# A fused attention and mixture-of-experts kernel: list scatters between splits, the first early list read sooner, mask made on chip, decays spread by TensorE, states ahead of transposes in steps 1 and 2

## The chip, the cores and the metric

The kernel runs on one core of a Trainium2 chip. The metric is the device time of one execution in microseconds (us), the median of the runs. TensorE is PE in the profile (its weight loads PEld), VectorE is DVE, ScalarE is ACT, GpSimd is POOL, and SyncE, which issues most of the DMAs, is SP. A shape such as 128x512 is partitions by elements.

## What is computed

Retention attention with a decay per head, and on its output a mixture of 16 experts in 4 groups, one expert for each token.

```python
# attention: B, H, S, D = 4, 8, 768, 64
gamma = 1 - 2.0 ** (-5 - arange(H)); scale = 1 / sqrt(D)
for t in range(S):
    state = gamma * state + outer(k[:, :, t], v[:, :, t])   # D x D a head
    y[:, :, t] = scale * q[:, :, t] @ state
# experts: x = y as (3072 tokens, 512); 4 groups of 4 experts, 512 -> 1024 -> 512
g = argmax(x @ w_group); e = argmax(x @ w_expert[g])        # and their softmax weights
out[token] = g_w * e_w * (relu(x[token] @ w1[g, e]) @ w2[g, e])
```

## The kernel before

**Attention.** The 768 positions of each of 4 sequences are 6 chunks of 128. Two sequences are worked on together, so there are 12 steps (`i`, 0 to 11), each with two halves `u`, one a sequence. A step computes scores (`score_mm`, L232, into the four PSUM banks `sh`), masks them with a triangle (`score_mask`, L244, `pf<-sh,cst`), scales the values (`vprep`, L191, POOL, `vs<-lv,cst`), transposes the keys of the next step on PE (`keys_mm`, L217), and accumulates in PSUM banks `op` the old state's part (`state_out`, L283) and the chunk's own part (`value_out`, L296). The state grows in `stp` (`state_mm`, L258). `out_x` (L308) multiplies by the decays `gx` of each position, and `trans_mm` (L342) turns the result so that it can be stored in DRAM as `xd`. `logits_mm` (L316) and `select_mm` (L329) give the router's logits.

**Routing.** Every second step a `route` of four chunks runs on DVE in small operations (L381 to L475), with ranks from PE (L429, L431). For each chunk an indirect DMA from POOL (`enlist`, L481, `meta<-src,slot`, a scatter) then writes 128 pairs of token and weight into the experts' lists in DRAM.

**Early experts.** Experts 0 (`ua`) and 1 (`va`) start before all tokens are routed: their first 128 tokens come out of the first 12 and 16 chunks. Their weights are loaded in 256 KB parts (`wload_part`, L666) and split in two 16-bit parts, `wh` on ACT (L678) and `wl` on POOL or DVE (L680). `listed` reads the list back (L693, `mt<-meta`), `gather` fetches the tokens (L703, `xg<-xd,mt`), `xtrans` turns them on PE (L721, `tpx`), and `layers` multiplies (L769 and on). After the attention PE works on `ua` while the last route runs, then on `va`, on the rest of both lists (`ub`, `vb`), and on the 14 other experts, the order of which is known only from the whole routing.

**What sets the order.** The program is in a manual schedule: each engine's instructions stand as the Python code emits them, and each queue is in order. `attention` writes a step out by hand; it calls `beside(i, place)` at places -1, 0, 2, 4, 1, 3 of step `i`, and `extra(i)` at its end, and these put the work for the early experts between. The table `NEXT` says at which place of which step the parts of `va`'s weights are loaded. `entries(n)` scatters the next `n` chunks.

**The start.** SP issues the first half of q, k and v, then the constants `cst` (the mask of 256 columns, the value scales, the step decays), then the second halves and the next steps' loads, among them the decays `gx<-dec` of 128x512. PE runs nine warming matmuls (L153), and after the first scores two more (`heat`, L171).

Of the kernel before, what the change touches and what calls it, by code (L numbers as in the profile page):

```python
# [22 lines left out]
P = 128  # L23
# [24 lines left out]

C_TRI, C_GV, C_GS, C_REST = 0, 256, 304, 308
C_STRI, C_DESC, C_SEL = 0, 128, 148  # L50
# [18 lines left out]
def constants():  # L69
    s = np.arange(P)  # L70
    g = 1.0 - 2.0 ** (-5.0 - np.arange(H))
    c = np.zeros((P, C_REST + C_END), np.float64)
    for i in range(2):
        c[:, C_TRI + i * P:C_TRI + i * P + P] = (s ^ (64 * i))[:, None] <= s[None, :]

    n = np.arange(NC)[None, :, None] * P + KEYS.T[:, None, :] + 1.0
    c[:, C_GV:C_GV + NC * H] = (g ** -n).reshape(P, NC * H)
    for half in range(2):
        c[64 * half:64 * half + 64, C_GS:C_GS + 4] = g[[h[half] for h in HEAD]] ** P
    d = c[:, C_REST:]  # L80
    d[:, C_STRI:C_STRI + P] = s[:, None] < s[None, :]
    d[:, C_DESC:C_DESC + 20] = [4, 3, 2, 1] * 5
    d[:, C_SEL:C_SEL + 20] = s[:, None] % 32 == np.arange(20)[None, :]
    d[:, C_SEG:C_SEG + NP] = np.arange(NP) * CAP
    d[:, C_KP:C_KP + NP] = np.arange(NP)
    d[:, C_WP:C_WP + NP] = PW
    d[:, C_IT:C_IT + MAXI] = np.arange(MAXI)
    return c.astype(np.float32)


def decays():
# [3 lines left out]
    a = g[:, :, None] ** (np.arange(P) + 1.0) * (XS / np.sqrt(D))  # L95
    return np.repeat(a.transpose(1, 0, 2)[:, None], D, 1).reshape(P, DM).astype(np.float32)


KX = (4, 6)
NEXT = {(9, 0): (0, 2), (9, 3): (2, 4), (10, 0): (4, 8), (11, 0): (8, 12)}  # L100
KEYED = (9, 10)


class Kernel:
    def __init__(self, tc, qkv, kt, wr, w1p, w2p, cst, dec, out):
# [3 lines left out]
        self.st = {}  # L109
        self.todo = []  # L110
        self.steps = []
        self.held = None
# [7 lines left out]
    def setup(self):  # L120
# [7 lines left out]
        self.load("v", 0, (0,))  # L128
        nc.sync.dma_start(self.cst, self.a_cst[:, 0:C_REST])
        act = cp.tile([P, 1], F32, name="act")  # L130
        nc.scalar.activation(act, self.ones[:, 0:1], AF.Copy)
        self.ident = cp.tile([P, P], F32, name="ident")
        make_identity(nc, self.ident)

        self.sh = [self.pp.tile([P, 512], F32, name=f"sh{i}", tag="big", bufs=3) for i in range(3)]
# [4 lines left out]
        nc.vector.memset(self.wr, 0.0)  # L140
        self.gx = cp.tile([P, NC, 4, P], F32, name="gx")
        self.stri = cp.tile([P, P], BF16, name="stri")
# [24 lines left out]

    def heat(self, n):

        for i in range(n):  # L170
            self.nc.tensor.matmul(self.sh[3], self.ones, self.one, start=True, stop=True)  # L171

    def load(self, name, i, us=(0, 1)):
# [18 lines left out]

    def decay_load(self):
        self.nc.sync.dma_start(self.gx[:, 0].rearrange("p g t -> p (g t)"), self.a_dec)

# [41 lines left out]
    def score_mask(self, i, u):  # L237
        nc, s = self.nc, self.st[i]
        pf = s["pf", u] = self.wp.tile([P, 2, 4, P], F32, name="pf", bufs=3)
        tri = self.cst[:, C_TRI:C_TRI + 2 * P].unsqueeze(1).broadcast_to([P, 2, 2 * P])  # L240
        for par in range(2):
# [743 lines left out]
    def attention(self, extra, beside):  # L985

        self.setup()
        for o in "qB0 kB0 vB0 q1 k1 d0 v1 q2 k2 w0 c0".split():
            n, us = int(o[-1]), {"A": (0,), "B": (1,)}.get(o[1], (0, 1))
            if o[0] == "d":  # L990
                self.decay_load()
            elif o[0] == "c":
                self.nc.sync.dma_start(self.rest, self.a_cst[:, C_REST:])
# [5 lines left out]
        def entries(n):  # L999
            for _ in range(min(n, len(self.todo))):  # L1000
                self.enlist(*self.todo.pop(0))

        def scores(i, u):
# [6 lines left out]
        self.vprep(0)  # L1010
        self.heat(2)
        self.outs(0)
# [6 lines left out]
        for i in range(NS2):  # L1019
# [9 lines left out]
            if i:  # L1029
                self.outs(i)  # L1030
                if i > 1:
                    scores(i + 1, 0)
                if i % 2 and not last:
                    self.select_late()
                self.state_out(i, 0)
                if last:
                    self.select_late()
                self.state_out(i, 1)
                self.select_late()
# [27 lines left out]
            if not last:  # L1067
                self.keys_mm(i + 1, banks=(self.log, self.sh[0]) if i < 2 else None)
                self.load("k", i + 4)
# [36 lines left out]
    def run(self):  # L1106
        tc, nc = self.tc, self.nc
        with ExitStack() as ctx:
# [35 lines left out]
            def extra(i):  # L1144
                early(i - 1, 1, False)
                for k in range(2):
# [4 lines left out]
            def beside(i, place):  # L1151

                last = i == NS2 - 1
                if last and place == -1:
                    assert self.done >= EARLY[1]
                    self.listed(va, "early1")
                for k in range(*NEXT.get((i, place), (0,))):
                    self.wload_part(va, k)
                if place == -1 and i == 10:
                    self.gather(ua)  # L1160
                if i == 9 and place == 1:
                    assert self.done >= EARLY[0]
                    self.listed(ua, "early0")
                if place == 0:
# [9 lines left out]
                if place == 2:  # L1174
                    if last:
                        self.xtrans(ua, 'big', (0,), low=False)
                        self.wsplit(va, 1, low=False)
                if place == 1:
                    early(i - 1, 0, False)
                    if last:  # L1180
# [177 lines left out]
```

## Time and profile before

| | us |
|---|---|
| median of 3 runs | 415.9 |
| the three runs | 415.9, 420.04, 410.48 |
| the profiled execution's own time | 414.41 |
| its span, first to last instruction | 412.7 |
| PE busy in the span | 393.4 (95%) |
| DVE, ACT, POOL busy | 289.3, 224.1, 169.9 |

The span lies 1.7 us under the profiled execution's own time. A row of the timeline gives the start, the duration, the engine, the line, what is written from what, how many instructions were merged, and in brackets how long the engine sat idle before and what ended that. Line numbers are those of the kernel before. In the changed kernel they are 3 to 5 higher for most of the helpers.

### The profile page before, as it was taken

What the parts mean: (1) busy time and instruction counts of PE and PEld (TensorE: products, weight loads), DVE (VectorE), ACT (ScalarE), POOL (GpSimd) and SP (SyncE); (2) the same over time, 40 slices, a digit from 0 to 9 for tenths busy, and PEclk for the clock granted to TensorE, in tenths of its full rate; (3) what the DMA queues carried; (4) which work ended last, traced back from release to release, by engine and by line L of the source; (5) the groups of instructions that cost most, each with busy time, mean ns of one, the idle gap of its engine ahead of it and who ended that gap; (6) DMA issues with size and microseconds to landing.
All of it is one profiled execution on the core that took longest, in us unless ns stands there. A gap on an engine that the chain in (4) does not pass through costs nothing.

```text
span 412.7 us, 13925 instructions
## 1 busy us (share of the span) xinstructions
PE 393.4 (95%) x5797; PEld 322.8 (78%) x5829; DVE 289.3 (70%) x480; ACT 224.1 (54%) x345; POOL 169.9 (41%) x152
## 2 busy tenths in 40 slices
PE   8999999998989999999999999999999999999990
PEld 4788888885757789595979788797887978879890
DVE  4565675668759558676999686877878769788620
ACT  2234534451654557555557666676766767667510
POOL 3455679687545230640507042350522504412001
PEclk9999999999999999999999999999999999999997
DMA  7999999996843986886887887979879798895001
GB/s 247 352 365 330 318 340 353 346 285 213 282 103 108 382 312 221 274 260 249 250 265 244 279 278 267 318 269 306 260 291 330 276 323 271 287 322 216 28 11 34
DMA packets 42300, 107.99 MB, mean 262 GB/s; under 512 B 14550, under 2 KB 14806, under 8 KB 35068
## 3 DMA queue, kind: packets, MB, share of 16 engines
q1 hardware_dynamic: 31260, 89.77, 64.4%
q0 software_dynamic: 10976, 17.31, 12.2%
q8 instruction: 47, 0.77, 0.7%
q14 instruction: 17, 0.14, 0.1%
HBM read 94.61 MB, written 13.73 MB: 262 GB/s over the span
## 4 chain that ended last, share of the span: by engine, by line
PE 52%; issue 29%; POOL 9%; DMA 4%; DVE 2%; ACT 1%; POOLq 0%; SPq 0%; ACTq 0%; DVEq 0%
PE hps L769 16%; PE yps L804 9%; POOL out L928 5%; PE op L296 4%; POOL xg L703 4%; PE yps L851 4%; PE sh L232 3%; PE yps L854 3%; PE op L283 2%; PE sh L342 2%; PE stp L258 2%; PE sh L316 2%; DMA xd<-xr 2%; DMA gx<-dec 2%; PE tpx L721 2%
## 5 line engine op out<-in xcount | busy, mean ns | idle before, releaser
L680 DVE TENSOR_TENSOR wl<-wf,wh 128x1024 bf16<-128x1024 f32 x120 | 147.8, 1243 | 35.9 <-ACT wh L678 32.8
L678 ACT ACTIVATE wh<-wf 128x1024 f16<-128x1024 f32 (+1 forms) x136 | 133.3, 1001 | 0.0
L769 PE MATMUL hps<-xbl,wh 128*128 128x128 f16 (+15 forms) x576 | 129.8, 245 | 1.8 <-PE log L431 1.2
L769 PE MATMUL hps<-xbh,wh 128*128 128x0 bf16 x576 | 127.5, 237 | 0.6 <-issue 0.6
L769 PE MATMUL hps<-xbh,wl 128*128 128x0 bf16 x576 | 127.5, 237 | 0.0
L928 POOL DMA_INDIRECT out<-yo,mt x32 | 40.8, 1275 | 162.2 <-ACT yo L910 134.3
L769 PEld LDWEIGHTS <-wh 128*128 128x128 f16 x1152 | 98.3, 98 | 3.3 <-issue 2.0
L703 POOL DMA_INDIRECT xg<-xd,mt x32 | 51.7, 1617 | 32.1 <-PE hps L769 21.9
L774 ACT ACTIVATE hh<-hps 128x256 bf16<-128x256 f32 (+15 forms) x72 | 34.9, 486 | 52.0 <-PE hps L769 41.6
L854 PEld LDWEIGHTS <-wh 128*128 128x128 f16 x704 | 42.7, 97 | 21.0
L769 PEld LDWEIGHTS <-wl 128*128 128x128 bf16 x576 | 56.3, 98 | 1.6 <-issue 0.9
L244 DVE TENSOR_TENSOR pf<-sh,cst 128x512 f32<-128x512 f32 x48 | 30.7, 684 | 28.0 <-PE sh L232 9.7
L777 DVE SCALAR_TENSOR_TENSOR hl<-hps,hh 128x256 f16<-128x256 f32 (+15 forms) x68 | 37.4, 551 | 10.1 <-ACT hh L774 9.1
L723 ACT ACTIVATE xbh<-tpx 128x512 bf16<-128x512 f32 (+14 forms) x32 | 16.8, 525 | 39.8 <-PE tpx L721 39.8
L851 PE MATMUL yps<-wh,hh 128*128 128x512 f16 x88 | 33.3, 379 | 0.0
L851 PE MATMUL yps<-wh,hl 128*128 128x512 f16 x88 | 33.3, 379 | 0.0
L851 PE MATMUL yps<-wl,hh 128*128 128x512 bf16 x88 | 33.2, 378 | 0.0
L191 POOL TENSOR_TENSOR vs<-lv,cst 128x512 f32<-128x512 f32 x24 | 24.6, 1045 | 20.8 <-DMA lv<-qkv 9.1
L481 POOL DMA_INDIRECT meta<-src,slot x24 | 23.9, 994 | 17.8 <-DMA lk<-qkv 6.0
L854 PEld LDWEIGHTS <-wl 128*128 128x128 bf16 x352 | 22.1, 97 | 10.5
L747 DVE TENSOR_TENSOR xbl<-tpx,xbh 128x512 f16<-128x512 f32 (+14 forms) x32 | 19.1, 598 | 14.7 <-ACT xbh L723 14.5
L854 PE MATMUL yps<-hl,wh 128*128 128x103 f16 (+10 forms) x352 | 26.2, 197 | 0.0
(168 smaller groups left out, 605.9 us busy)
## 6 DMA issues: line engine op xcount, KB each, us to landing
wf<-w1p SPq DMA_DIRECT2D x26, 1024.0 KB
wf<-w2p SPq DMA_DIRECT2D x26, 1024.0 KB
lq<-qkv SPq DMA_DIRECT2D x24, 256.0 KB
lk<-qkv SPq DMA_DIRECT2D x24, 256.0 KB
lv<-qkv SPq DMA_DIRECT2D x24, 256.0 KB
xd<-xr SPq DMA_DIRECT2D x22, 256.0 KB
wf<-w1p SPq DMA_DIRECT2D x16, 256.0 KB
wf<-w2p SPq DMA_DIRECT2D x16, 256.0 KB
```

The lines of the kernel that those rows point to most:

```text
L191: self.nc.gpsimd.tensor_tensor(o, v, g, ALU.mult)
L244: nc.vector.tensor_tensor(o, sc, tri, ALU.mult)
L678: nc.scalar.activation(u["wh"][i][:, cs], u["wf"][i][:, cs], AF.Copy)
L680: (eng or nc.vector).tensor_tensor(u["wl"][i][:, cs], u["wf"][i][:, cs], u["wh"][i][:, cs], ALU.subtract)
L703: nc.gpsimd.indirect_dma_start(out=xg[0:r, i, :], out_offset=None, in_=self.xd[0:n, :], in_offset=bass.IndirectOffsetOnAxis(ap=mt[0:r, i, ...
L769: nc.tensor.matmul(o, l[:, k, fs], m, start=(n == 0), stop=(n == 11), skip_group_check=True)
L774: nc.scalar.activation(hh[:, f, 0:W], hv[:, :, 0:W], AF.Relu)
L777: nc.vector.scalar_tensor_tensor(*rest)
L804: nc.tensor.matmul(ps[0:r, :], l[:, k, ts], m[k], start=(n == 0), stop=(n == 23))
L851: nc.tensor.matmul(big, h[:, k, 0:P], w[k], start=(n == 0), stop=(n == 23))
L854: nc.tensor.matmul(o, w[k][:, d * P:d * P + P], m, start=(n == 0 and d == 0), stop=(n == 23), skip_group_check=True,)
L928: s = nc.gpsimd.indirect_dma_start(out=self.out, out_offset=bass.IndirectOffsetOnAxis(ap=mt[0:r, i, 0:1].bitcast(U32), axis=0), in_=yo[0:r ...
```

## The change

- The mask is made on POOL (`tri`: a memset and three `affine_select`), and is no longer loaded. `cst` shrinks from 308 columns (154 KB) to 52 (26 KB), and is loaded from ACT's queue.
- The decays are loaded as 2 rows of 512, with a 2x128 selector beside them (5 KB, ACT's queue), into a piece of `gx` that is overwritten later. One matmul spreads them over 128 partitions into the bank `sh[3]` and ACT copies them to `gx`. The two `heat` matmuls and the 256 KB load go.
- In step 1 all of `state_out` stands between the two halves of the key transposes; in step 2 its first half stands ahead of the transposes of step 0's output.
- In steps 10 and 11 the two splits of `ua`'s weights on POOL stand after the first and the second of four scatters.
- `listed(ua)` moves from place 1 to place 2 of step 9, and two of `va`'s weight loads from place 0 to place 2, behind it.

```diff
@@ setup
-        nc.sync.dma_start(self.cst, self.a_cst[:, 0:C_REST])
+        self.gx = cp.tile([P, NC, 4, P], F32, name="gx")
+        self.dec = self.gx.rearrange("p c g t -> p (c g t)")[0:2, DM:2 * DM + P]
+        nc.scalar.dma_start(self.cst, self.a_cst[:, 0:C_REST])
+        nc.scalar.dma_start(self.dec, self.a_dec)
...
+        self.tri = cp.tile([P, 2, P], F32, name="tri")
+        nc.gpsimd.memset(self.tri, 1.0)
+        for i, a, b, base in ((0, 0, P, 0), (1, 0, 64, -64), (1, 64, P, 0)):
+            tri = self.tri[a:b, i, :]
+            nc.gpsimd.affine_select(
+                out=tri, in_=tri, compare_op=ALU.is_ge, fill=0.0, base=base, pattern=[[1, P]], channel_multiplier=-1
+            )
@@ helpers
-    def decay_load(self):
-        self.nc.sync.dma_start(self.gx[:, 0].rearrange("p g t -> p (g t)"), self.a_dec)
+    def decay_first(self):
+
+        self.nc.tensor.matmul(self.sh[3], self.dec[:, DM:], self.dec[:, 0:DM], start=True, stop=True)
+        self.nc.scalar.activation(self.gx[:, 0].rearrange("p g t -> p (g t)"), self.sh[3], AF.Copy)
...
-        tri = self.cst[:, C_TRI:C_TRI + 2 * P].unsqueeze(1).broadcast_to([P, 2, 2 * P])
+        tri = self.tri.rearrange("p i t -> p (i t)").unsqueeze(1).broadcast_to([P, 2, 2 * P])
@@ attention
-        for o in "qB0 kB0 vB0 q1 k1 d0 v1 q2 k2 w0 c0".split():
+        for o in "qB0 kB0 vB0 q1 k1 v1 q2 k2 w0 c0".split():
...
                 self.enlist(*self.todo.pop(0))
+                if self.between:
+                    self.between.pop(0)()
...
-        self.heat(2)
+        self.decay_first()
...
             if i:
-                self.outs(i)
+                if i > 2:
+                    self.outs(i)
...
-                self.state_out(i, 0)
+                if i > 2:
+                    self.state_out(i, 0)
                 if last:
                     self.select_late()
-                self.state_out(i, 1)
+                if i > 1:
+                    self.state_out(i, 1)
...
-                self.keys_mm(i + 1, banks=(self.log, self.sh[0]) if i < 2 else None)
+                banks = (self.log, self.sh[0]) if i < 2 else None
+                if i == 0:
+                    self.keys_mm(1, (0,), banks)
+                    self.outs(1)
+                    self.state_out(1, 0)
+                    self.state_out(1, 1)
+                    self.keys_mm(1, (1,), banks)
+                else:
+                    self.keys_mm(i + 1, banks=banks)
+                if i == 1:
+                    self.outs(2)
+                    self.state_out(2, 0)
@@ run
-NEXT = {(9, 0): (0, 2), (9, 3): (2, 4), (10, 0): (4, 8), (11, 0): (8, 12)}
+NEXT = {(9, 2): (0, 2), (9, 3): (2, 4), (10, 0): (4, 8), (11, 0): (8, 12)}
...
             def extra(i):
-                early(i - 1, 1, False)
+                if i < 10:
+                    early(i - 1, 1, False)
...
+                if i == 9 and place == 2:
+                    assert self.done >= EARLY[0]
+                    self.listed(ua, "early0")
                 for k in range(*NEXT.get((i, place), (0,))):
                     self.wload_part(va, k)
...
-                if i == 9 and place == 1:
-                    assert self.done >= EARLY[0]
-                    self.listed(ua, "early0")
...
+                if place == 0 and i >= 10:
+                    self.between = [lambda k=k: early(i - 1, k, False) for k in range(2)]
                 if place == 1:
-                    early(i - 1, 0, False)
+                    if i < 10:
+                        early(i - 1, 0, False)
```

Three places show how instructions move. On PE in step 1, before (`log` and `sh_109` are the banks of the key transposes, `op` that of the outputs):

```order
L217 MATMUL log<-ident,lk 128x128 x4
L217 MATMUL sh_109<-ident,lk 128x128 x4
L283 MATMUL op<-lq,V 64x128 x16
L296 MATMUL op<-pf,vs 64x128 x16
L258 MATMUL stp<-vs,kk 64x64 x16
```

and now:

```order
L222 MATMUL log<-ident,lk 128x128 x4
L288 MATMUL op<-lq,V 64x128 x16
L222 MATMUL sh_116<-ident,lk 128x128 x4
L301 MATMUL op<-pf,vs 64x128 x16
L263 MATMUL stp<-vs,kk 64x64 x16
```

The old state's product now stands ahead of the transposes into the score bank. On POOL in steps 10 and 11, before (`wl` is a split, `meta` a scatter, `xg` a gather):

```order
L703 DMA xg_80<-xd,mt 128x512
L481 DMA meta<-src_127,slot 57600x2 x4
L680 TENSOR_TENSOR wl<-wf,wh 128x512 x3
L703 DMA xg_80<-xd,mt 128x512
L680 TENSOR_TENSOR wl<-wf,wh 128x512
L481 DMA meta<-src_129,slot 57600x2 x4
L481 DMA meta<-src_131,slot 57600x2 x4
```

and now:

```order
L708 DMA xg_80<-xd,mt 128x512
L486 DMA meta<-src_133,slot 57600x2
L685 TENSOR_TENSOR wl<-wf,wh 128x512
L486 DMA meta<-src_133,slot 57600x2
L685 TENSOR_TENSOR wl<-wf,wh 128x512
L486 DMA meta<-src_133,slot 57600x2 x2
L708 DMA xg_80<-xd,mt 128x512
L486 DMA meta<-src_135,slot 57600x2
L685 TENSOR_TENSOR wl<-wf,wh 128x512
L486 DMA meta<-src_135,slot 57600x2
L685 TENSOR_TENSOR wl<-wf,wh 128x512
L486 DMA meta<-src_135,slot 57600x2 x2
```

A split now parts the first three scatters of each step; the last step's four (`src_137`, behind these) stay together. On SP around step 9, before (`mt` is the list that is read back, its second row a lone transfer of 128x2):

```order
L666 DMA wf<-w1p 128x512 x2
L666 DMA wf<-w2p 128x512 x2
L693 DMA mt<-meta 128x2
L209 DMA kk<-kt 128x512 x2
L353 DMA xd<-xr 128x512 x2
L666 DMA wf<-w1p 128x512 x6
```

and now:

```order
L671 DMA wf<-w2p 128x512 x2
L698 DMA mt<-meta 128x2
L671 DMA wf<-w1p 128x512 x2
L214 DMA kk<-kt 128x512 x2
L358 DMA xd<-xr 128x512 x2
L671 DMA wf<-w1p 128x512 x6
```

The list is read two loads sooner, and these two loads now wait on SP behind it.

## Rows read from the trace of the kernel before

**Rows 1.** Stretch, us, busy PE, PEld, DVE, ACT, POOL (instructions), clock, DMA share, GB/s:

```profile
157.00:403.00 246.00, 246.00 (x3070) 202.59 (x3093) 187.63 (x232) 154.12 (x215) 79.28 (x52) 1.00 0.75 255
116.00:157.00 41.00, 40.01 (x540) 30.89 (x543) 29.59 (x58) 23.55 (x40) 16.17 (x17) 1.00 0.62 223
8.00:14.00 6.00, 5.74 (x159) 5.02 (x156) 2.30 (x4) 1.19 (x2) 1.04 (x1) 1.00 1.00 376
```

**Rows 2.** Timeline of PE in steps 0 to 2:

```profile
6.15 0.60 PE L171 MATMUL sh<-const-bfloat16-1.0,ones 128*128 128x512 bf16 x2
7.33 1.09 PE L296 MATMUL op<-pf,vs 128*64 128x128 f32 x16 [0.59 <-POOL vs L191]
...
10.72 1.09 PE L296 MATMUL op<-pf,vs 128*64 128x128 f32 x16 [0.27 <-POOL vs L191]
...
14.93 0.66 PE L217 MATMUL sh<-ident,lk 128*128 128x128 f32 x4 [0.56 <-DVE pf L244]
...
22.92 1.25 PE L342 MATMUL sh<-ident,xt 128*128 128x128 f32 x8 [0.38 <-DVE pf L244]
```

**Rows 3.** Timelines of DVE and POOL in the first 14 us:

```profile
6.22 1.29 DVE L244 TENSOR_TENSOR pf<-sh,cst 128x512 f32<-128x512 f32 x2 [2.69 <-DMA cst<-cst]
...
12.99 1.29 DVE L308 TENSOR_TENSOR xt<-op,gx 128x512 f32<-128x512 f32 x2 [2.38 <-DMA gx<-dec]
...
9.63 1.04 POOL L191 TENSOR_TENSOR vs<-lv,cst 128x512 f32<-128x512 f32 x1 [2.35 <-DMA lv<-qkv]
```

**Rows 4.** DMA issues by line: out<-in, queue, count, KB each:

```profile
gx<-dec SPq DMA_DIRECT2D x1, 256.0 KB
cst<-cst SPq DMA_DIRECT2D x1, 154.0 KB
```

**Rows 5.** Timeline of PE at the end of steps 8, 9, 10 and 11:

```profile
78.17 0.52 PE L258 MATMUL stp<-vs,kk 128*64 128x64 f32 x12
...
81.11 1.09 PE L342 MATMUL sh<-ident,xt 128*128 128x128 f32 x8
...
87.57 1.10 PE L258 MATMUL stp<-vs,kk 128*64 128x64 f32 x32
...
89.17 1.09 PE L342 MATMUL sh<-ident,xt 128*128 128x128 f32 x8
...
95.79 1.05 PE L258 MATMUL stp<-vs,kk 128*64 128x64 f32 x20
...
101.42 1.09 PE L342 MATMUL sh<-ident,xt 128*128 128x128 f32 x8
...
115.82 0.22 PE L769 MATMUL hps<-xbl,wh 128*128 128x128 f16 x1 [1.18 <-PE log L431]
```

**Rows 6.** Timeline of POOL from step 10 on:

```profile
93.49 1.08 POOL L703 DMA_INDIRECT xg<-xd,mt  x1 [2.35 <-DMA mt<-meta]
95.13 1.01 POOL L481 DMA_INDIRECT meta<-src,slot  x1 [0.56 <-DVE nb L472]
...
100.02 2.28 POOL L680 TENSOR_TENSOR wl<-wf,wh 128x512 bf16<-128x512 f32 x2
...
121.30 0.98 POOL L481 DMA_INDIRECT meta<-src,slot  x1 [0.30 <-issue]
```

**Rows 7.** Timeline of SP's DMA issues in steps 9 and 10:

```profile
87.80 0.33 SPq L693 DMA_DIRECT2D mt<-meta  x1
88.72 0.81 SPq L209 DMA_DIRECT2D kk<-kt  x2
...
91.41 4.20 SPq L666 DMA_DIRECT2D wf<-w1p  x6
```

**Rows 8.** DVE's splits: all (ns min/median/max), and the one beside POOL's two:

```profile
L680 DVE TENSOR_TENSOR wl<-wf,wh x120: 1202/1224/4052, 99.3 to 389.5; 128x1024 bf16<-128x1024 f32 x120
...
99.34 4.05 DVE L680 TENSOR_TENSOR wl<-wf,wh 128x1024 bf16<-128x1024 f32 x1
```

**Rows 9.** Timeline of PE where the first tokens of `ub` are turned:

```profile
132.21 0.60 PE L721 MATMUL tpx<-ident,xg 128*128 128x128 f32 x4
```

More of the change, by code (lines that the diff above doesn't have):

```diff
@@ L46 @@
 PW = WIDTH + [P] * 3 + [P + LATE]
-C_TRI, C_GV, C_GS, C_REST = 0, 256, 304, 308
+C_GV, C_GS, C_REST = 0, 48, 52
 C_STRI, C_DESC, C_SEL = 0, 128, 148
@@ L72, in constants @@
     c = np.zeros((P, C_REST + C_END), np.float64)
-    for i in range(2):
-        c[:, C_TRI + i * P:C_TRI + i * P + P] = (s ^ (64 * i))[:, None] <= s[None, :]
     n = np.arange(NC)[None, :, None] * P + KEYS.T[:, None, :] + 1.0
@@ L95, in decays @@
     a = g[:, :, None] ** (np.arange(P) + 1.0) * (XS / np.sqrt(D))
-    return np.repeat(a.transpose(1, 0, 2)[:, None], D, 1).reshape(P, DM).astype(np.float32)
+    half = np.repeat(np.eye(2), D, 1)
+    return np.concatenate([a.transpose(1, 0, 2).reshape(2, DM), half], 1).astype(np.float32)
 KX = (4, 6)
-NEXT = {(9, 0): (0, 2), (9, 3): (2, 4), (10, 0): (4, 8), (11, 0): (8, 12)}
+NEXT = {(9, 2): (0, 2), (9, 3): (2, 4), (10, 0): (4, 8), (11, 0): (8, 12)}
 KEYED = (9, 10)
@@ L110, in __init__ @@
         self.todo = []
+        self.between = []
         self.steps = []
@@ L140, in setup @@
         nc.vector.memset(self.wr, 0.0)
-        self.gx = cp.tile([P, NC, 4, P], F32, name="gx")
         self.stri = cp.tile([P, P], BF16, name="stri")
@@ L166, in clear_lists @@
         )
-    def heat(self, n):
-        for i in range(n):
-            self.nc.tensor.matmul(self.sh[3], self.ones, self.one, start=True, stop=True)
     def load(self, name, i, us=(0, 1)):
@@ L987, in attention @@
         self.setup()
-        for o in "qB0 kB0 vB0 q1 k1 d0 v1 q2 k2 w0 c0".split():
+        for o in "qB0 kB0 vB0 q1 k1 v1 q2 k2 w0 c0".split():
             n, us = int(o[-1]), {"A": (0,), "B": (1,)}.get(o[1], (0, 1))
-            if o[0] == "d":
-                self.decay_load()
-            elif o[0] == "c":
+            if o[0] == "c":
                 self.nc.sync.dma_start(self.rest, self.a_cst[:, C_REST:])
```

## The prediction, made before the result was known

> **What bounds it now.** I read the busy time by stretches first. From 157 to 403 us PE is busy for all of 246.00 us, and from 116 to 157 us for 40.01 of 41.00, at a granted clock of 1.00 [rows 1]. So nothing after 116 us waits for more than 1 us in all, and what PE has to do there is not changed. Whatever moves PE's arrival at 116 us moves the end by as much, if lists, weights and splits move with it. The change is therefore priced in the first 116 us, by PE's gaps in the timeline and by stretches where the same instructions took longer than in another step.
>
> At the start the gaps are 0.59, 0.27, 0.56 and 0.38 us [rows 2]. Behind them stand DVE, which waited 2.69 us for `cst` and 2.38 us for the decays, and POOL, which waited 2.35 us for the second half of v [rows 3]. The DMA engines are full there (share 1.00, 376 GB/s from 8 to 14 us) [rows 1].
>
> At the end of each step PE does `state_mm` (32 matmuls) and the logits (8), up to the output transposes at L342. In step 9 this took 89.17 - 87.57 = 1.60 us; in step 8, 81.11 - 78.17 = 2.94; in step 10, 101.42 - 95.79 = 5.63 [rows 5]. Step 9 has no scatter near, step 8 has two, a split, two and a split, and step 10 has four back to back from 95.13 until the splits at 100.02 [rows 6]. In step 10 SP also issues six weight loads just before, from 91.41 on [rows 7]. The excess over step 9 is 1.34 us in step 8 and 4.03 in step 10. The rows do not tell whether scatters or loads make it. At 115.82 PE waited another 1.18 us, again just behind four scatters [rows 5].
>
> **Constants and decays.** 128 KB of `cst` leave SP's queue ahead of the second halves (154 KB become 26) [rows 4]. At 376 GB/s [rows 1] that is 0.35 us for every load behind it. PE's second wait, at 10.72, ends with POOL's scaling, which starts when v has landed at 9.63 [rows 2, 3]: with v 0.35 us sooner PE goes on 0.35 us sooner. The first wait (0.59) also shrinks, since the mask no longer comes by DMA, but what it saves is spent waiting at the second, so the two together are worth 0.35. Bounds: nothing, if the two small loads on ACT's queue delay v by as much, and 0.86, both gaps gone. I take 0.35, since the v that ends the wait is still behind five other loads.
>
> The 256 KB of decays leave too, 0.70 us of DMA time. The values of step 1 land sooner, which covers the earlier start of their product. The spreading matmul takes the place of two bf16 matmuls that are 0.60 us together [rows 2]; in fp32 the nearest row has 16 matmuls of 128 columns in two half-arrays in 1.09 us [rows 2], so 512 full columns are 0.5 us or a little more. PE would wait for `vs` then anyway: nothing. ACT's copy and POOL's mask fall where both engines are idle.
>
> What a page has to say: by the Trainium skill, DMA: Bandwidth & Descriptors, Specifications, transfers under 512 B run below line rate, since the engine reads, modifies and writes. The rows of `cst` fall from 1,232 to 208 B. No row here shows a load of such rows ahead of the first use; if it lost all that the smaller size saves, the sum would be 0.35 us less.
>
> **States ahead of transposes.** In step 1 PE waits 0.56 us at 14.93 for DVE to mask the bank into which it transposes, DVE being late because the decays held `out_x` until 12.99 [rows 2, 3]. Now 16 matmuls stand between and DVE is sooner: 0.56 gone. In step 2, 0.38 us at 22.92 goes in the same way [rows 2]. Late next would be the scaled values of step 1; with v no sooner at all they would be ready about when PE is. Bounds for both together: nothing, and 0.94. I take 0.94. The start is 0.35 + 0.94 = 1.3 us.
>
> **Scatters between splits.** The price lies between nothing (loads make the excess) and 4.03 - 1.34 = 2.69 us (scatters do, and step 10 becomes as step 8) [rows 5], plus up to 1.18 in step 11. A longer stall is bounded below, with the rivals. I take half of each, as nothing tells the two causes apart: 1.35 + 0.6 = 1.95 us. The splits cost POOL 2.28 us [rows 6] between scatters instead of behind them; the last four scatters stand behind the two splits of step 11, and end about 0.4 us later against PE than before. They end at 122.3, and PE wants the gathered tokens at 132.21 [rows 6, 9]: covered by the room in that chain of list, gather and landing; without it 0.4.
>
> DVE's split at 99.34 took 4.05 us where the median is 1.22, beside POOL's two at 100.02 [rows 6, 8]. The splits now run beside other work of DVE, in step 11 beside the last route's small operations. I count nothing for it, since those are short and most read PSUM; what it costs if they are held too is rival 5.
>
> **The list sooner.** The gather of `ua` waited 2.35 us for the list [rows 6], but POOL's next scatter waited for DVE anyway (0.56) [rows 6], and PE uses these tokens 10 us later: nothing. The two loads behind it feed a split on ACT, of which DVE makes its part only at 99.34 [rows 8]: nothing.
>
> **The sum.** 414.4 - 1.3 - 1.95 = 411.1 us for an execution like the profiled one, whose own time is 1.5 under the median of the three. So I expect 412.6 as a median. The three runs spread over 9.6 us, so about 2%, or 8.3 us, is what a measurement can tell from no change.
>
> **Rivals.**
> 1. The loads, not the scatters, make the stall of step 10. For it: six of them in 4.2 us [rows 7]. Against it: the wait at 115.82 stands behind four scatters too. Then only the start pays: 414.4 - 1.3 = 413.1, as a median 414.6.
> 2. The scatters make all of it. For it: back to back costs three times what pairs cost. Then 414.4 - 1.3 - 2.69 - 1.18 = 409.2, as a median 410.7.
> 3. Slower: SP stands at the list until the twelfth chunk's scatter has landed (87.80), then issues the two moved loads, and only then the keys of step 10 (88.72 before) [rows 7]. 512 KB at 376 GB/s [rows 1] put 1.4 us ahead of the keys, and PE wants them 1.3 us sooner, at 94.5 instead of 95.79 [rows 5]. The list, issued at 87.80, was used at 93.49: 5.7 us under load [rows 6, 7]. Keys issued at 89.6 would land at 95.3, and with 1.4 us more ahead of them at 96.7. It decides once they land after 94.5. At 2.2 us it takes more than the start's gain, and PE stands in the very stretch that the scatters' relief was to shorten, so nothing of that is left: 414.4 - 1.3 + 2.2 = 415.3, as a median 416.8. Against it: SP has by then issued nothing for two microseconds, so the queue is emptier.
> 4. The change does not do what it says at the start: the values of steps 1 and 2 land no sooner, and PE's gaps move from DVE to POOL. Then 414.4 - 1.95 = 412.5, as a median 414.0.
> 5. POOL's splits hold DVE in step 11. For it: the one split of DVE that ran beside POOL's two took 2.83 us more than the median [rows 8]. If the last route is held for the 2.28 us of two splits [rows 6], its scatters and lists are late by that and the 0.4 us above, and if the chain to 132.21 [rows 9] has no room, PE too: 414.4 - 1.3 - 1.95 + 2.7 = 413.9, as a median 415.4. Against it: the route's operations before the ranks come from PSUM. The Trainium skill, GPSIMD Engine Reference, Key points, has the rule: GpSimd shares its SBUF interfaces with VectorE and contends with instructions that have two SBUF inputs. The row at 99.34 agrees with it, and it speaks against moving splits to where DVE is on the path.
>
> **Chances.** Forecast 0.4, loads 0.25, scatters 0.15, keys late 0.1, no start 0.05, DVE held 0.05. The cases lie between 410.7 and 416.8, and a median of three moves by some 2 us by itself. I give 408.5 to 417.5; this leaves out the unlucky end of the keys' case and the lucky end of the scatters'. Faster by over 2% is under 407.6, slower is over 424.2; all my cases lie within, and only the runs' own spread reaches outside: faster 0.06, same 0.91, slower 0.03.
>
> **What would show it.** Right: no wait of PE on DVE's masks up to 24 us, so that 14.93 and 22.92 come 0.9 and 1.3 us sooner; PE's stretch from `state_mm` to L342 in step 10 falls from 5.63 to 3 or 4 us; DVE's longest split falls under 2.5 us; PE is as full as before from 116 us on. Wrong: waits for `vs` in step 1, for `kk` in step 10, or a step 10 as long as before. I should be off most if the spread of the runs is itself the stalls near the scatters: then a change that removes them moves the median by more than one trace shows.

## The result, and the profile of the changed kernel

The change took 413.96 us as a median of 22 runs, the kernel before 413.79 of 22 on the same chip. The ratio of change to before is 1.0052, 95% interval 1.0029 to 1.0074. The ratios, here and below, are of the fast runs alone, without the executions over 1.5% above the fastest of their kernel; over all 22 the two medians are level. In two further comparisons the ratio was 1.003 (0.9991 to 1.0068) and 1.005 (1.0018 to 1.0083). By these ratios the change is 0.3 to 0.5% slower, 1 to 2 us, where 0.8% faster (412.6 against 415.9) was forecast: the time lies in the range, the sign is wrong. That the time comes near the forecast is luck: 412.6 was counted from the median of three runs, 415.9, and over 22 the kernel before takes 413.79. The profiled execution is 413.66 us long, 0.8 less than the one of before; as will be seen, one execution says little here.

Stretches of the change (columns as in [rows 1]):

```profile
157.00:403.00 246.00, 245.87 (x3068) 202.36 (x3091) 187.37 (x232) 154.05 (x215) 79.58 (x52) 1.00 0.75 255
116.00:157.00 41.00, 36.85 (x490) 28.28 (x493) 26.91 (x45) 21.67 (x35) 19.75 (x18) 1.00 0.64 228
8.00:14.00 6.00, 6.00 (x166) 5.22 (x162) 3.96 (x7) 1.28 (x3) 3.50 (x4) 1.00 1.04 368
```

The start is full now, 6.00 of 6.00 us. The new hole is the middle row: 36.85 us busy of 41.00, against 40.01 in [rows 1]. PE of the change, start to the first tokens of `ub` (start us, busy us; in brackets the wait and what ended it):

```profile
6.20 1.12 PE L198 MATMUL sh<-gx 2*128 2x512 f32 x2
7.25 1.09 PE L301 MATMUL op<-pf,vs 128*64 128x128 f32 x16
...
13.74 1.31 PE L288 MATMUL op<-lq,V 64*64 64x128 f32 x32
14.99 0.66 PE L222 MATMUL sh<-ident,lk 128*128 128x128 f32 x4
...
22.09 1.10 PE L347 MATMUL sh<-ident,xt 128*128 128x128 f32 x8
...
94.97 0.98 PE L263 MATMUL stp<-vs,kk 128*64 128x64 f32 x28
...
97.79 1.09 PE L347 MATMUL sh<-ident,xt 128*128 128x128 f32 x8
...
100.56 0.66 PE L726 MATMUL tpx<-ident,xg 128*128 128x128 f32 x4
...
114.98 0.66 PE L726 MATMUL tpx<-ident,xg 128*128 128x128 f32 x4 [3.15 <-DMA xg<-xd,mt]
...
132.41 0.63 PE L726 MATMUL tpx<-ident,xg 128*128 128x128 f32 x4 [3.64 <-DMA xg<-xd,mt]
```

The waits of [rows 2] are gone, and step 2's transposes stand at 22.09 instead of 22.92. Five us later nothing is left of this gain, since a gap of 1.25 us stands there for which the profile names no cause ("issue"). The change:

```profile
26.17 0.90 PE L237 MATMUL sh<-lq,lk 64*64 64x128 f32 x31 [1.25 <-issue]
27.00 1.97 PE L301 MATMUL op<-pf,vs 128*64 128x128 f32 x32
```

and the kernel before, in which the same product stood at 26.96:

```profile
26.96 1.97 PE L296 MATMUL op<-pf,vs 128*64 128x128 f32 x32
```

The stretch of step 10 (94.97 to 97.79) is 2.8 us instead of 5.63 [rows 5]. At the tokens of `ua` (100.56) PE is 3.6 us ahead of before (104.19). At the tokens of `va` it waits 3.15 us, at those of `ub` 3.64, and there it stands at 132.41, where it stood before at 132.21 [rows 9]: all of the gain is given back. What it waits for is a chain on POOL:

```profile
100.47 0.98 POOL L486 DMA_INDIRECT meta<-src,slot  x1 [0.30 <-issue]
108.32 1.05 POOL L708 DMA_INDIRECT xg<-xd,mt  x1 [6.87 <-DMA mt<-meta]
109.67 0.99 POOL L486 DMA_INDIRECT meta<-src,slot  x1 [0.30 <-DVE sms L415]
110.69 1.17 POOL L685 TENSOR_TENSOR wl<-wf,wh 128x512 bf16<-128x512 f32 x1
112.03 1.00 POOL L486 DMA_INDIRECT meta<-src,slot  x1 [0.17 <-issue]
113.03 1.18 POOL L685 TENSOR_TENSOR wl<-wf,wh 128x512 bf16<-128x512 f32 x1
...
122.85 0.98 POOL L486 DMA_INDIRECT meta<-src,slot  x1 [0.30 <-issue]
128.11 1.91 POOL L708 DMA_INDIRECT xg<-xd,mt  x1 [4.28 <-DMA mt<-meta]
```

POOL idles 6.87 us before the gather of `va` (108.32), then puts the two splits between the scatters of step 11. Its eight scatters take 14.2 us (109.67 to 123.83) and end 1.5 us later than before, 122.28 [rows 6]. List and gather of `ub` follow in a row, and PE stands at the end of them. SP stands too: its last four loads of `w2p` go into a buffer that these splits of `ua`'s weights must have read. SP of the change from 106 to 118 us, what it waited for (us in total, times, longest):

```profile
SPq L671 <- POOL wl L685: 4.3, 1, 4.3
```

In the four executions of the change that were profiled this wait is 3.0 to 4.3 us, in the three without alternation (below) there is none. It did not reach PE: apart from its wait at `ub`, PE went from the tokens of `va` to those of `ub` in 13.8 us in all four.

### The profile page after: what moved, and what is told of

Its sections match the earlier page's. It is cut to its first block, busy times and chain, and to the rows that moved or that the text cites. A ratio compares the mean times of both kernels' runs of the same rounds, so it can differ in the third digit from the quotient of the medians.

```text
span 412.0 us, 13934 instructions
## 1 busy us (share of the span) xinstructions
PE 389.8 (95%) x5797; PEld 322.7 (78%) x5829; DVE 288.5 (70%) x480; ACT 225.2 (55%) x346; POOL 174.5 (42%) x156
## 4 chain that ended last, share of the span: by engine, by line
PE 46%; issue 16%; POOL 6%; DMA 1%; DVE 0%; ACT 0%; POOLq 0%
PE hps L774 21%; PE yps L856 9%; PE yps L809 7%; PE yps L859 5%; POOL out L933 3%; PE tpx L726 2%; POOL xg L708 2%; POOL meta L486 1%; DMA xg<-xd,mt 1%; PE yps L881 1%; PE tpy L928 1%; DVE wl L685 0%; ACT wh L683 0%; POOLq L933 0%; POOLq L708 0%
## 5 line engine op out<-in xcount | busy, mean ns | idle before, releaser
L685 DVE TENSOR_TENSOR wl<-wf,wh 128x1024 bf16<-128x1024 f32 x120 | 144.9, 1219 | 35.9 <-ACT wh L683 35.6
L933 POOL DMA_INDIRECT out<-yo,mt x32 | 40.9, 1277 | 159.8 <-ACT yo L915 132.5
L708 POOL DMA_INDIRECT xg<-xd,mt x32 | 52.7, 1645 | 34.2 <-PE hps L774 16.5
L249 DVE TENSOR_TENSOR pf<-sh,tri 128x512 f32<-128x512 f32 x48 | 30.7, 685 | 28.8 <-PE sh L237 14.3
L486 POOL DMA_INDIRECT meta<-src,slot x24 | 25.9, 1081 | 15.2 <-issue 4.1
L859 PE MATMUL yps<-hl,wh 128*128 128x103 f16 (+10 forms) x352 | 26.2, 197 | 0.0
```

What stands on the lines that cost most here:

```text
L249: nc.vector.tensor_tensor(o, sc, tri, ALU.mult)
L486: i = nc.gpsimd.indirect_dma_start(out=self.metaf, out_offset=bass.IndirectOffsetOnAxis(ap=slot[:, c:c + 1], axis=0), in_=src[:, c, :], in ...
L685: (eng or nc.vector).tensor_tensor(u["wl"][i][:, cs], u["wf"][i][:, cs], u["wh"][i][:, cs], ALU.subtract)
L708: nc.gpsimd.indirect_dma_start(out=xg[0:r, i, :], out_offset=None, in_=self.xd[0:n, :], in_offset=bass.IndirectOffsetOnAxis(ap=mt[0:r, i, ...
L859: nc.tensor.matmul(o, w[k][:, d * P:d * P + P], m, start=(n == 0 and d == 0), stop=(n == 23), skip_group_check=True,)
L933: s = nc.gpsimd.indirect_dma_start(out=self.out, out_offset=bass.IndirectOffsetOnAxis(ap=mt[0:r, i, 0:1].bitcast(U32), axis=0), in_=yo[0:r ...
```

## The experiments

The theory under test is the queue theory: POOL's order of scatters and splits sets when the lists are read, and these set PE at the tokens of `ub`. The rivals are that the start or the sooner list costs what the change lost, or that the trace's differences are accidents of one execution. Ratios are to the kernel before, with 95% intervals.

### The change without its alternation

`e1_none` keeps start and list, and puts the splits back. It was run three times, twice beside the change on one chip.

```diff
             def extra(i):
-                if i < 10:
-                    early(i - 1, 1, False)
+                early(i - 1, 1, False)
...
-                if place == 0 and i >= 10:
-                    self.between = [lambda k=k: early(i - 1, k, False) for k in range(2)]
                 if place == 1:
-                    if i < 10:
-                        early(i - 1, 0, False)
+                    early(i - 1, 0, False)
```

> The change without its alternation: scatters of steps 10 and 11 back to back and the splits behind them, as before; start, mask, decays and the sooner list are kept. Chain theory (POOL's order of scatters and splits sets when the lists are read, and the lists set PE from 112 us on): PE's stretch state_mm to L347 of step 10 is again 5 to 5.6 us, but the scatters of step 10 end near 100.0 (101.45 with alternation), the gather of va's tokens starts near 106.8, and PE waits less than 1 us in all before tpx(va) and tpx(ub), against 3.15 + 3.64; tpx(ub) at 131.0 to 131.6; time 0.5 to 1.2 us below the kernel before, 0.1 to 1 below the change. Rival (the alternation is good, and the start or the moved list costs what it gains): the long stretch of step 10 returns with nothing given back, tpx(ub) at 134 to 135, time 2 to 3 us above the change.

> e1_none once more (start and sooner first list, no alternation), beside h2_start_timed, which has the list as before: the difference is the list's. Queue theory: the list of ua has room (gather at 90 to 93, tpx(ua) at 98 to 104), so within 0.002 of h2_start_timed. Rival: the sooner list and the later w1p loads cost or give 0.3% or more.

> Start and sooner first list without alternation, a third time, beside the change on one chip: so far 0.9964 and 0.9972 of the kernel before. If these stand: 0.994 to 0.999 again, and 0.4 to 0.9% below i2_change_third. Rival: within 0.3% of the change.

The change beside it:

> The change itself, timed beside the next three on one chip. Sum of the parts so far: start 0.996, alternation in steps 10 and 11 together 0.005 to 0.009 on top (e1_none 0.9964 against the change 1.0052): ratio to the kernel before 1.001 to 1.006, and 0.5 to 1% above h2_start_timed. Rival (the differences are those of chips and calls): within 0.002 of h2_start_timed.

> The change, a third time, beside i1_none_third: so far 1.0052 and 1.003 of the kernel before. If the alternation is what it loses by: 1.001 to 1.006 again. Rival: 0.999 or less.

Measured without alternation: 0.9964 (0.9916 to 1.0012), 0.9972 (0.9933 to 1.0011), 0.996 (0.993 to 0.999). The change beside the second and third: 1.003 and 1.005, the medians 412.92 against 411.01 and 413.98 against 410.20 us. So the alternation is what the change loses by, 0.5 to 0.9%. **Without it the kernel is faster than the change**, and it lies 0.3 to 0.4% below the kernel before in all three comparisons, though two of the three intervals reach past 1. Against the start alone, timed on the same chip, the change is 0.3% slower (the start's 1.0001 is below), where 0.5 to 1% was expected and at most 0.2% by the rival. Two things came out otherwise than the chain theory had it: the long stretch of step 10 did not return, and PE still waits, 4.59 us at `va`, where under 1 us in all was expected. PE of `e1_none`:

```profile
95.80 1.28 PE L263 MATMUL stp<-vs,kk 128*64 128x64 f32 x32 [0.43 <-DMA kk<-kt]
97.02 0.64 PE L321 MATMUL sh<-xt,wr 128*32 128x256 f32 x8
97.59 1.09 PE L347 MATMUL sh<-ident,xt 128*128 128x128 f32 x8
...
116.21 1.12 PE L726 MATMUL tpx<-ident,xg 128*128 128x128 f32 x4 [4.59 <-DMA xg<-xd,mt]
...
131.37 0.60 PE L726 MATMUL tpx<-ident,xg 128*128 128x128 f32 x4
```

1.8 us from `state_mm` to the transposes, with scatters back to back. At `va` it waits longer than the change, at `ub` not at all: its eight scatters of step 11 take 10.1 us (110.60 to 120.68).

### Both kernels profiled a second time

> The kernel before once more, for a second profiled execution. Scatter theory (the scatters and splits behind them make the long stretch of step 10): state_mm to L342 of step 10 is again 5 to 6 us, the gaps of PE in it again 1 us or more, and no wait of PE over 1 us at tpx(va) or tpx(ub). Rival (the stretch is an accident of one execution, or of kk and the loads): the stretch is 2 to 4 us, as in the kernel without alternation (2.2 with its own wait for kk taken off).

PE and POOL of the kernel before, unchanged, in another execution:

```profile
97.34 1.10 PE L258 MATMUL stp<-vs,kk 128*64 128x64 f32 x32
98.37 0.64 PE L316 MATMUL sh<-xt,wr 128*32 128x256 f32 x8
98.94 1.09 PE L342 MATMUL sh<-ident,xt 128*128 128x128 f32 x8
103.67 0.66 PE L721 MATMUL tpx<-ident,xg 128*128 128x128 f32 x4 [1.89 <-DMA xg<-xd,mt]
...
118.23 0.66 PE L721 MATMUL tpx<-ident,xg 128*128 128x128 f32 x4 [3.30 <-DMA xg<-xd,mt]
...
133.54 0.60 PE L721 MATMUL tpx<-ident,xg 128*128 128x128 f32 x4
```

```profile
98.51 1.01 POOL L481 DMA_INDIRECT meta<-src,slot  x1 [0.31 <-issue]
...
112.39 1.00 POOL L481 DMA_INDIRECT meta<-src,slot  x1 [0.17 <-issue]
...
117.56 0.98 POOL L481 DMA_INDIRECT meta<-src,slot  x1 [0.30 <-issue]
...
121.42 1.96 POOL L481 DMA_INDIRECT meta<-src,slot  x1 [0.30 <-issue]
```

The stretch of step 10 is 1.60 us: the 5.63 us of [rows 5] were an accident of one execution, and the rival held. Of the scatters this execution says little, since the first of step 10 stands at 98.51, when all but 0.4 us of the stretch is over. That they do not make it is seen in the five executions that keep the kernel before's order on POOL (three of `e1_none`, two of the start alone): there four scatters back to back run beside the stretch, and it takes 1.8 to 3.0 us. The waits that were absent in the first trace are here (1.89 at `ua`, 3.30 at `va`). And the last four scatters (from 117.56) follow at once; DVE's split of step 10 takes 1.21 us.

> The change once more, for a second profiled execution. Queue theory: waits of PE at tpx(va) or tpx(ub) of 2.5 us or more in sum are there again, and the last scatter ends at 122 to 124.5. Rival (they were an accident of one execution, as the long stretch of step 10 was in the kernel before): under 1.5 us in sum.

The change again: 1.76 us at `va`, 0.91 at `ub`, in sum 2.67, and the last scatter ends at 122.77. The waits are there, at less than half the size.

### One step at a time, and the alternation alone

`e2_step10` has `i == 10` in place of `i >= 10` and `i != 10` in place of `i < 10`; `e3_step11` accordingly; `f4_alternate_only` is the kernel before with `between` and nothing else.

> The change with the alternation in step 10 alone; in step 11 one split stands ahead of the gather of va's tokens and one behind it, as before. Chain theory: tpx(va) as late as in the change (near 115.0, wait of 3 us), but the last scatter ends 1.2 to 2.4 us sooner than 123.83, and tpx(ub) stands at 130.3 to 131.3 against 132.41, with PE's wait there 1.5 to 2.5 us against 3.64; time 1 to 2 us below the change. Rival: tpx(ub) within 0.5 us of the change and the time too.

> The change with the alternation in step 11 alone; in step 10 scatters back to back, splits behind. Chain theory: stretch of step 10 again 5 to 5.6 us; list of va read near 103 and gather near 107, tpx(va) without a wait of PE over 1 us near 114 to 115; the scatters of step 11 end at 123 to 124 as in the change, since the two splits stand among them; tpx(ub) at 131.5 to 132.5; time within 0.7 us of the change. Rival (alternation good): time 0.5 us or more below that of the kernel with no alternation at all.

> The kernel before with the alternation of scatters and splits in steps 10 and 11 alone; constants, mask, decays, order of states and the first list as before. Scatter theory: step 10's stretch falls from 5.6 to 2.5 to 3.5 us, and PE then waits 2.5 to 4 us at tpx(ub), since the last scatter ends at 123.5 to 124.5. Rival (the sooner list and the moved w1p loads shortened the stretch): the stretch stays at 5 us or more with the alternation, tpx(ub) stands at 133 or later. Time by both within 1 us of the kernel before, or up to 1.5 above.

Ratios 1.001 (0.9968 to 1.0052), 1.0023 (0.9984 to 1.0062) and 1.0019 (0.9983 to 1.0054). All lie above the three of `e1_none`, but the intervals overlap: how the loss divides between the steps is open. In the trace of `e2_step10` there is no wait at `ub` (129.11); the time, forecast 1 to 2 us below the change, fits, but 1.5 to 2.5 us of wait at `ub` were expected. In the trace of `e3_step11` (417.22 us, the longest of its twelve executions) one scatter held POOL for 4.31 us, and PE waited 4.08 at `ub`, to 133.82, where 131.5 to 132.5 was expected; its stretch of step 10 is 1.83 us, not 5 to 5.6. `f4_alternate_only` refuted both of its cases: its stretch of step 10 is 1.6 us, and its wait at `ub` 0.35, since it had lost time at `va` first.

### A dose on POOL ahead of the last scatters

```diff
             for _ in route:
                 pass
+            for _ in range(4):
+                self.decay_next(1)
             while self.todo:
                 self.enlist(*self.todo.pop(0))
```

> The kernel e1_none (the change without alternation) with four extra products of 128x512 on POOL right ahead of the last four scatters, about 4.2 us; they write again what stands there. Queue theory (POOL's order ahead of the last scatters sets ub's list, and that list sets PE at tpx(ub)): last scatter 3.5 to 4.5 us later than in e1_none, PE waits 1 us or more at tpx(ub), time 1.5 to 4 us above e1_none, ratio to the kernel before 1.001 to 1.006. Rival (ub's list has room for it): no wait at tpx(ub), ratio within 0.002 of e1_none (0.9964).

Ratio 1.0144 (1.0092 to 1.0197), some 7 us above `e1_none`. POOL, then PE, of the dose:

```profile
114.00 6.13 POOL L204 TENSOR_TENSOR gx<-gx,cst 128x512 f32<-128x512 f32 x4
...
124.97 1.38 POOL L486 DMA_INDIRECT meta<-src,slot  x1 [0.30 <-issue]
```

```profile
134.17 1.09 PE L726 MATMUL tpx<-ident,xg 128*128 128x128 f32 x4 [5.40 <-DMA xg<-xd,mt]
```

The products took 6.13 us, not 4.2, and most of it arrives at PE as a wait of 5.40, with a slower clock behind it (0.50 from 132 to 136 us). Work of POOL ahead of the last scatters is paid for at PE: this is the queue theory's test, and it holds, a size above the forecast (at most 4 us). The dose is not quite clean: DVE's three splits beside it took 5.99 us in sum, against 3.5 in the other executions, so a part of the 7 us may be DVE's.

### The start alone

> The kernel before with only the start of the change: mask on chip, decays spread by TensorE, states ahead of the transposes in steps 1 and 2. Queue theory (what comes later than the end of step 8 is bound by lists, landings and PE together, and PE's gain of 0.9 us at 23 us is handed on only where PE is what comes last): time 0 to 1.3 us below the kernel before, ratio 0.997 to 1.000. Rival (the start costs what the change lost): ratio 1.003 or more.

> The kernel before with only the start of the change, once more, as the one part that pays: ratio to the kernel before 0.994 to 0.999. Rival: 1.000 or more, the 0.996 was chance.

0.996 (0.9929 to 0.999), then 1.0001 (0.9961 to 1.0041), the rival of the second expectation. The start shows no cost, and gives between nothing and 1.7 us. The traces show little of it: the product of step 2 that stands at 27.00 in the change stands at 27.0 in the mean of all seventeen executions with the new start (26.2 to 27.8), and at 27.2 in three with the old one (27.0 to 27.5). The sooner list on top of it (0.9964, and 0.9972 beside the second) makes no difference that these runs can tell, at most 0.3%, where 0.2% was expected.

### Splits where POOL waits anyway

```diff
                 if place == 0 and i >= 10:
-                    self.between = [lambda k=k: early(i - 1, k, False) for k in range(2)]
+                    for k in range(2):
+                        early(i - 1, k, False)
```

> The change with both pairs of splits ahead of the scatters: in step 10 right behind the gather of ua's tokens, in step 11 ahead of the gather of va's tokens, where POOL waited 3.12 and 6.87 us. Chain theory: scatters of step 10 end at 99.0 to 100.0 (101.45), of step 11's first four at 113 to 114 (116.65), the last at 119 to 121 (123.83); stretch of step 10 stays under 3.5 us; tpx(ub) at 128.5 to 130 against 132.41; time 2.5 to 4 us below the change and the kernel before. Rival (splits on POOL stretch VectorE's routing ops, so that slots come later): L451 to L477 of step 10 end at 95.5 to 96.5 instead of 94.3, or an op of the route takes over 1 us; time within 1 us of the change.

0.9976 (0.9935 to 1.0018). The splits run at 91.65 and 100.92, the last scatter ends at 117.3 (123.83), and nothing waits at `ub`; but PE waits 2.56 us at `va`, its clock falls (0.60 from 116 to 120 us), and it stands at `ub` at 130.45. That is 1 us below the kernel before and 2 to 3 below the change, where 2.5 to 4 below both were expected.

> The start of the change, and of step 11 both splits ahead of the gather of va's tokens, where POOL waits for the list, so that one split less stands ahead of the last scatters. Queue theory: last scatter 1 to 1.3 us sooner than in h2_start_timed, time 0 to 1.2 us below it (only executions in which ub's list comes last gain). Rival (splits beside VectorE's routes of step 11 stretch an op of the route, so that the slots are later): the same or up to 1 us above.

0.9988 (0.9945 to 1.0031): its last scatter ends at 116.2, 4 us before that of `h2_start_timed`, not 1 to 1.3; but PE waited 4.71 us at `va`. Scatters that end sooner than those of `e1_none` (120.68) bring nothing that these runs can tell: in these traces PE is held one gather earlier, at `va`.

### The gather of `va` and the loads beside it

SP issues four `w2p` loads (1 MB) behind the read of `va`'s list (104.73 in the change), then the `xd` stores, which wait for PE's transposes. The theory here is that a faster PE brings these transfers to the DMA engines ahead of the gather. `f2_w2p_late` is the change without `(11, 0): (8, 12)` in NEXT, and `for k in range(8, 16)` where it had `range(12, 16)`; `f3_ahead_w2p` is the same on `e4_ahead`; `g2_ahead_split_w2p` issues the last four only behind `self.listed(us[1])`.

> The change, with the four w2p loads of step 11 (1 MB) issued together with the next four, behind the xd stores and so behind the gather of va's tokens. Collision theory (PE comes 3 us sooner, so the xd stores and w2p loads stand in the DMA engines ahead of the gather): xg(va) lands 3.5 to 5 us after its issue (6.6 in the change), tpx(va) waits at most 1 us (3.15), and PE stands at tpx(ub) for 4.5 to 6.5 us instead of 3.64, because that list is as late as before; time within 1 us of the change. Rival (the list itself, read at 104.3, is what is late): xg(va) and the wait of 3 us stay within 0.7 us.

> Both edits: the splits ahead of the scatters in steps 10 and 11 (e4_ahead) and the four w2p loads behind the gather of va's tokens. Collision theory: xg(va) lands 3.5 to 5 us after issue (9.4 in e4_ahead), PE waits at most 1 us at tpx(va), its granted clock stays at 0.95 or more from 112 to 120 (0.60 in 116:120 of e4_ahead), tpx(ub) stands at 126.5 to 128 against 130.45, waiting at most 1.5 us; time 2 to 3.5 us below e4_ahead, 3 to 5 below the kernel before. Rival (w2p is then late, or another wait takes over): PE waits 2 us or more at tpx(ub) or in the layers of va, time within 1 us of e4_ahead.

> The splits ahead of the scatters and the w2p loads behind the gather, as in f3_ahead_w2p, but the second four w2p loads (1 MB) only after the lists of ub and of the first two shared units are read. Queue theory: no scatter of step 11 lasts 4 us (114.65 to 118.76 in f3_ahead_w2p), the last ends at 117 to 118.5 (121.03), xg(ub) lands at 126 to 127.5 (128.70), PE waits under 0.7 us at tpx(va) and under 1.8 us at tpx(ub) (3.06); time 1 to 3 us below f3_ahead_w2p and below the kernel before. Rival (the later w2p holds the split of va's last weights or the weights of the first shared unit): a new wait of PE of 1 us or more behind 135 us, time as f3_ahead_w2p or above.

`f2_w2p_late`, 1.0068 (1.0027 to 1.011): a miss. The loads came out beside the gather (both issued at 107.58), and the wait at `va` was 3.80. In `f3_ahead_w2p` they came 1.4 us behind it, and there PE does not wait at `va`. PE and POOL:

```profile
112.01 0.63 PE L726 MATMUL tpx<-ident,xg 128*128 128x128 f32 x4
...
128.83 1.07 PE L726 MATMUL tpx<-ident,xg 128*128 128x128 f32 x4 [3.06 <-DMA xg<-xd,mt]
```

```profile
106.85 1.05 POOL L708 DMA_INDIRECT xg<-xd,mt  x1 [3.84 <-DMA mt<-meta]
...
114.65 3.81 POOL L486 DMA_INDIRECT meta<-src,slot  x1 [0.30 <-issue]
118.76 0.98 POOL L486 DMA_INDIRECT meta<-src,slot  x1 [0.30 <-issue]
```

Half of the expectation: the wait at `va` is gone, but a scatter holds POOL for 3.81 us while the eight loads run, and the wait stands at `ub`: 1.0006 (0.9967 to 1.0046). Two more executions show the same: where PE waited nothing at `va` (`i1_none_third`) and 0.63 us (`e3_step11`), a scatter held POOL for 4.17 and 4.31 us, and PE waited 4.09 and 4.08 at `ub`. (The first execution of the kernel before, with PE late, waits at neither.) `g2_ahead_split_w2p` took the loads from that place and lost 2.5% (1.0246), as PE shows:

```profile
138.56 0.61 PE L809 MATMUL yps<-wh,hh 128*128 128x512 f16 x1 [9.55 <-ACT hh L779]
```

ACT stood 13.07 us at the split of `va`'s fourth tile, waiting for `w2p`, and what PE wanted of ACT stood behind it. The list chain was as sought (last scatter ended at 118.3), and no time says what it would be worth.

## Why the prediction was wrong

**Bound and condition: right, but the condition was not met.** "Whatever moves PE's arrival at 116 us moves the end by as much, if lists, weights and splits move with it": behind the tokens of `ub` all is indeed rigid. PE's end is 270.4 to 270.9 us away from there in the fourteen executions in which its clock stayed at 1.00 behind that place, and 272.1 to 273.3 in those in which it fell (`g2_ahead_split_w2p`, held later, is left out). The lists did not move with PE: they came later.

**Start: right in place, not shown in size.** The waits went where it was said: step 1's new row at 13.74 leaves the transposes of 14.99 without a wait, and in none of the seventeen executions with the new start does PE wait for DVE or POOL up to 24 us. But 14.93 did not come 0.9 us sooner, since the old state's product now stands ahead of it, and of the 1.3 us forecast PE had gained 0.83 at 22.09, nothing at 27.00, and 0.2 at that place in the mean: gaps without a named cause come in instead. The timed runs leave it open: alone the start is 0.996 and 1.0001, with 0.997 forecast. The small loads on ACT's queue did not hold it up: POOL's first scalings wait for v alone. What the Trainium skill says of transfers under 512 B (DMA: Bandwidth & Descriptors, Specifications) has no visible price here.

**The step that failed** is "Scatters between splits", at two places. First "I take half of each ... 1.35 + 0.6 = 1.95 us" priced a stretch of 5.63 us that only the first execution had: 1.60 in the second of the same kernel, 1.8 to 3.0 in the five without alternation that have the new start, 2.2 to 3.5 in the four of the change. So scatters back to back do not make it, and neither do the six loads, which were issued ahead of it in all of them; rivals 1 and 2 fall as well. What stopped PE in that one execution, its rows do not name. Second, and this is what made the sign: "the last four scatters ... end about 0.4 us later against PE than before ... covered by the room in that chain". The eight scatters of step 11 take 13.3 to 14.2 us in the change's four executions, and 10.1 in two of the three without alternation (13.6 in the third, where one of them held POOL for 4.17): 3 to 4 us more, not 0.4, and no room. About 2.1 us of this are the two splits; the other 1.2 to 2.0 are one or two scatters that held POOL for up to 2.0 us, for which the rows name no cause. The room was read from the same odd execution, in which PE's ranks came late to DVE and POOL's last four scatters waited for the last route. DVE, then POOL, of the kernel before:

```profile
116.14 0.23 DVE L439 TENSOR_TENSOR log<-log,nb 128x64 f32<-128x64 f32 x1 [1.99 <-PE log L431]
```

```profile
117.45 0.98 POOL L481 DMA_INDIRECT meta<-src,slot  x1 [2.42 <-DVE rows L464]
```

Without that delay they follow at once, as in the second execution, and every split between them is added. PE waited at `ub` in all four executions of the change (3.64, 0.91, 0.85 and 2.25 us), in neither of the kernel before, in the third one without alternation, for 4.09, and in one of the two of the start alone, for 0.89.

Not all is accounted for. That the alternation costs time is shown by taking it out; that it costs it at `ub` is argued from these waits and the dose. The timed runs put 0.5 to 0.9% between the change and `e1_none`, while their profiled executions reach `ub` 0.9 us apart in the mean and end 0.3 us apart, with a spread of 6 us; how much of the loss is waiting at `ub`, at `va` or for the clock, seven traces can't say.

**The list sooner**: nothing that the runs can tell, as forecast. **Rival 3** (keys late) was right in its mechanism: PE waits for `kk` in step 10, 0.2 to 2.2 us, in ten of the fourteen executions with the sooner list, with or without alternation, and in none of the six with the list as before. No price of it shows at the end: 0.9972 with the sooner list, 1.0001 without. **Rival 5** came nearest, with the right chain and about the price (2.7 us late lists) but the wrong cause. An operation of the last route was held in three of the four executions of the change; DVE of the first:

```profile
110.00 1.89 DVE L423 TENSOR_SCALAR u<-sms 128x4 f32<-128x4 f32 x1
```

It takes 0.16 to 0.20 us in the other three; in two of them an operation with two SBUF inputs took 1.84 and 1.50, and each of the three ends with a split of POOL. DVE's split of step 10, which was to stay under 2.5 us, took 2.88 in two of the four. But in all of them POOL's last four scatters followed the four before them at once: its queue was late without it. So the rule of the Trainium skill on shared SBUF interfaces (GPSIMD Engine Reference, Key points) fits the rows with two SBUF inputs (the row above has one) without deciding the time: what delayed the scatters was POOL's own queue, its splits and its longer scatters.

## What to carry to other kernels

A stall that stands in one execution is not yet a cost of the program: look for it in a second execution before pricing an edit by it, and do not take slack from that execution either, because a late engine makes room in every chain beside it. Work put between the links of a chain of transfers lengthens the chain by its whole time; look for a place where the queue waits (here that brought no more than taking the work out), and ask which chain ends last once PE is sooner. Where two gathers in a row hold PE, an edit that frees one shows up as a wait at the next.

## What the runs showed of the chip

- PE's granted clock can fall to its lower level behind a wait. Stretches of `e2_step10` around PE's wait of 3.15 us at `va`, which ended at 112.57 (columns as in [rows 1]):

```profile
112.00:116.00 4.00, 3.21 (x9) 1.81 (x12) 1.65 (x2) 2.28 (x4) 2.98 (x4) 0.50 0.95 303
116.00:120.00 4.00, 4.00 (x14) 1.59 (x13) 3.81 (x10) 1.25 (x2) 2.95 (x2) 0.68 0.09 24
```

0.50 is 1.2 GHz. From `va` to `ub` PE needs 13.8 us without such a fall (the change, its wait at `ub` taken off) and 16.5 here, so it cost 2.7 us on top of the wait. The change's own wait of 3.15 us left the clock at 1.00.
- A scatter holds POOL for 0.98 us as a rule, but 1.8 to 2.0 once or twice in most executions, and 3.81, 4.17 and 4.31 in three, each time 3 to 7 us after SP began to issue loads of `w2p`; other executions had such loads and no such scatter.
- The fp32 matmul that spreads the decays from two partitions took 1.12 us (two records of 512 columns, 6.20), not the 0.5 or a little more estimated from half-array rows; ACT's copy waited 0.45 us for it, PE did not.
- POOL's products of 128x512 took 1.5 us each in the dose, beside DVE's work, where 1.05 is their time at the start.
